# A fused state-space convolution and attention kernel: another order of the setup, fifteen angles and complex products, ranked streams, and shorter VectorE passes

## The chip, the cores and the metric

The kernel runs on one core of a Trainium2 chip. The core has five engines with their own instruction queues: TensorE (PE) for matmuls, VectorE (DVE), ScalarE (ACT), GpSimd (POOL) and SyncE (SP); the last two here only start DMA transfers. The metric is the device time of one execution in microseconds, the median over runs; lower is better.

## The reference

Two independent results are put side by side in the output.

```python
# a: a diagonal state-space model, D = 576 channels, N = 128 states, L = 2048 positions
P = exp(dt * A * l);  K[d, l] = Re( sum_n C[d,n] * P[d,n,l] * dt * B[d,n] )
a = causal_convolution(u, K) + u * Dskip          # over rfft/irfft of length 2L
# b: attention with 32 query heads of 18, and one key and one value head; S = 2048
q = x @ wq;  k = x @ wk;  v = x @ wv
b = softmax(q k^T / sqrt(18)) v  @ wo
out = concat([a, b], -1)
```

## The kernel before, in words

**Attention.** Four chunks of 512 queries, 16 pairs of heads in each, 16 blocks of 128 keys: 1024 score steps. A step is two matmuls of one head each (`s`, two times 128 keys x 512 queries, float16 operands in two parts), one exponential on ScalarE of 128 x 1024 (`P`, lines 741 and 743), and its share of the product with the values (`ops`, float32, four column groups at once). Scores have three PSUM buffers, so they are issued in groups of three; the exponentials of a group free the buffers for the next. Between groups TensorE does other work through one PSUM bank (`bank`): products, query projections (`q`), output projections (`op`), and the matmuls of the convolution. Whatever goes through that bank has to be copied out by VectorE before the next can begin.

**Convolution.** Twelve groups of 48 channels. For each, `factors` builds powers of exp(dt A) for 26 positions a channel and state: a magnitude (an exponential on ScalarE) times a cosine and a sine (two ScalarE sine passes); `tables` multiplies them up to a table `tab` of 2 x 24 x 96 for each half group, `kgen` (`kg`) contracts the table over states on TensorE into the filter. The input and the filter are transformed by matmuls with DFT matrices (`hu`, `lu`, `hk`, `lk`), multiplied with a three-way splitting on VectorE and by accumulating DMAs (`spectrum`, `back`), and transformed back (`iy`). Two channel groups share one turn of sines: the second one's arrays are parked in DRAM and fetched back. Since an exponential and a sine need different ScalarE tables, a turn is: two exponentials over 1248 elements, later a table load, four sines of 1248, a table load. There are five such turns in the loop and one in the setup.

**What sets the order.** `build` writes the order of PE, ACT, DVE and POOL by hand, by a planner that keeps an estimated clock for every engine. `main` goes through the score steps; in front of each group `fill` asks the streams for work until the score buffers are expected free. The convolution has four streams (`fronts`, `inputs`, `kernels`, `backs`); `Conv.go` advances the one that has spent the least VectorE work so far. Constants at the head of the file hold the planner's prices and thresholds.

**The setup.** It loads weights and x, projects the first queries (`kq`, copied to `qc`), places them (`rows`), projects keys (`kv`) and values (`pv`) for the whole sequence in four column groups, and places the first keys (`kaug`). It also runs the arguments and sines of the first two channel groups. The bound on the scores needs the keys' maxima (`km`, `kmx`, `kmax`) and a matmul `up`. After the first two scores the loop places the second keys (`kp`), finishes the value projection, transposes the values (`vp`) to `v_sb`, and computes the other four maxima (`kmx`, four 128-wide matmuls).

## Time and profile before

| | |
|---|---|
| runs | 1161.06, 1162.67, 1165.83 us; median 1162.67 |
| profiled execution | 1167.64 us; its span, first to last instruction, 1165.9 us |
| busy PE, ACT, DVE, POOL | 1102.5, 1038.6, 924.4, 97.4 us (95%, 89%, 79%, 8%) |
| mean granted TensorE clock | 0.988 |
| DMA | 123.93 MB, a mean of 106 GB/s |

A row of the groups reads: line, engine, operation, output and inputs with shapes, count, then busy time and mean duration in ns, then the engine's idle time just before and who ended it. A line number is often that of a helper (291 is the one that records every matmul, 326 the two-operand VectorE operation), so the names tell the groups apart. A float32 matmul shows as two rows of the profile. A row of the timeline starts with the start in us from the span's beginning and the time until the last of the merged instructions ends; the next one can start a little before that. In brackets stands the idle time in front.

### The profile page before, as it was taken

To read this page: it belongs to the slowest core of one execution; us is meant where nothing else is said; L and a number is where in the kernel's file an instruction comes from. 1 tells how busy PE (TensorE), PEld (TensorE's weight loads), DVE (VectorE), ACT (ScalarE), POOL (GpSimd) and SP (SyncE) were. 2 spreads that over 40 slices of the span, in tenths; PEclk is the share of its full clock that TensorE was granted. 3 is DMA by queue.
4 is the path that set the end of the run, shared out by engine and by line. 5 is a ranking of instruction groups with operands and counts; after the bars stand their busy time and mean duration, and the time that the engine had idled before them with its cause. 6 is when DMAs were issued, how large, how long until landed. Compare 5 with 4: busy or idle time off the path is not lost. (4 is left out here: it accounts for less than half of the span.)

```text
span 1165.9 us, 42886 instructions
## 1 busy us (share of the span) xinstructions
PE 1102.5 (95%) x18790; PEld 563.4 (48%) x18790; DVE 924.4 (79%) x1649; ACT 1038.6 (89%) x1092; POOL 97.4 (8%) x151
## 2 busy tenths in 40 slices
PE   7999999999998899999899999899999899998997
PEld 2454554454445455455444445455455455554444
DVE  7686886985896896797997697896799888796643
ACT  5798999999987999899998998999999999997983
POOL 2001110201010100010120000000110100000000
PEclk9899999999998999999999999999999999999999
DMA  8323261524242353143554133352234252243141
GB/s 307 125 70 117 85 171 52 164 76 124 89 115 79 129 125 112 43 96 99 155 141 154 47 66 94 126 127 99 84 67 139 77 154 83 72 95 99 47 91 57
DMA packets 55026, 123.93 MB, mean 106 GB/s; under 512 B 7500, under 2 KB 24925, under 8 KB 53555
## 3 DMA queue, kind: packets, MB, share of 16 engines
q1 hardware_dynamic: 43571, 87.44, 21.7%
q0 software_dynamic: 10832, 33.27, 13.5%
q8 instruction: 149, 2.44, 0.9%
q10 hardware_dynamic: 432, 0.44, 0.1%
q14 instruction: 42, 0.34, 0.1%
HBM read 53.47 MB, written 41.46 MB: 81 GB/s over the span
## 5 line engine op out<-in xcount | busy, mean ns | idle before, releaser
L743 ACT ACTIVATE P<-s 128x1024 f32<-128x1024 f32 x992 | 942.0, 1027 | 91.3 <-PE s L291 87.3
L291 PE MATMUL ops<-P,v_sb 128*32 128x256 f32 (+1 forms) x9008 | 550.2, 364 | 8.1 <-DVE o L330 6.0
L291 PEld LDWEIGHTS ops<-P,v_sb 128*32 128x32 f32 x9008 | 271.5, 110 | 218.5 <-issue 74.6
L291 PE MATMUL s<-aug,kaug 55*128 55x512 f16 x2048 | 292.7, 381 | 11.3 <-ACT P L743 5.8
L291 PEld LDWEIGHTS <-kaug 55*128 55x128 f16 x2048 | 95.0, 94 | 185.1 <-issue 137.6
L291 PE MATMUL op<-wo_sb,oT 126*32 126x288 f32 (+1 forms) x1120 | 85.4, 428 | 8.7 <-DVE ob L330 5.1
L291 PE MATMUL q<-x,wq_sb 128*32 128x256 f32 x1360 | 87.1, 388 | 6.2 <-DVE ql L346 3.9
L291 PEld LDWEIGHTS q<-x,wq_sb 128*32 128x32 f32 x1360 | 42.2, 111 | 41.4 <-issue 16.9
L326 DVE TENSOR_TENSOR tab<-tab,tt 128x576 f32<-128x576 f32 (+1 forms) x72 | 59.1, 821 | 1.8
L326 DVE TENSOR_TENSOR tab<-tab 128x576 f32<-128x576 f32 (+1 forms) x72 | 58.6, 814 | 0.0
L326 DVE TENSOR_TENSOR ks<-ks 128x384 f32<-128x384 f32 (+2 forms) x84 | 55.1, 668 | 1.6
L291 PEld LDWEIGHTS op<-wo_sb,oT 126*32 126x32 f32 (+1 forms) x1120 | 35.3, 114 | 43.0 <-issue 10.2
L276 POOL DMA_DIRECT2D qd<-qh x46 | 26.0, 578 | 322.7 <-DVE qh L334 322.7
L291 PE MATMUL kg<-tab 128*32 128x64 f32 x2304 | 42.9, 224 | 9.7 <-DVE us L326 7.5
L326 DVE TENSOR_TENSOR acc<-acc 128x768 f32<-128x768 f32 (+1 forms) x48 | 40.2, 854 | 11.3 <-DMA acc<-t 10.5
L291 PEld LDWEIGHTS kg<-tab 128*32 128x32 f32 x2304 | 36.8, 112 | 23.9 <-issue 15.2
L326 DVE TENSOR_TENSOR t<-us,ks 128x1728 f32<-128x1728 f32 (+2 forms) x36 | 47.2, 1347 | 0.0
L334 DVE TENSOR_SCALAR qh<-q 128x256 f16<-128x256 f32 x34 | 14.1, 416 | 37.3 <-PE q L291 37.3
L741 ACT ACTIVATE P<-s,nb 128x1024 f32<-128x1024 f32 x32 | 33.3, 1114 | 8.1 <-PE s L291 8.0
L276 POOL DMA_DIRECT2D ks<-ks x12 | 11.0, 914 | 332.9 <-DVE ksb L330 224.4
L330 DVE COPY ksb<-kg 128x192 f32<-128x192 f32 x48 | 17.2, 359 | 26.5 <-PE kg L291 26.5
L326 DVE TENSOR_TENSOR us<-us 128x384 f32<-128x384 f32 (+1 forms) x60 | 37.1, 633 | 1.0
(356 smaller groups left out, 1076.7 us busy)
## 6 DMA issues: line engine op xcount, KB each, us to landing
park<-two SPq DMA_DIRECT2D x6, 1944.0 KB
acc<-t POOLq DMA_DIRECT2D x12, 864.0 KB, 6.8
od<-o SPq DMA_DIRECT2D x31, 256.0 KB
acc<-t POOLq DMA_DIRECT2D x12, 576.0 KB, 5.7
aug<-qd SPq DMA_DIRECT2D x124, 54.0 KB
u<-u SPq DMA_DIRECT2D x12, 384.0 KB
kd<-ksb SPq DMA_DIRECT2D x12, 384.0 KB
kt<-kd SPq DMA_DIRECT2D x48, 96.0 KB
```

The source lines that it names most:

```text
L276: return self.q.dma_start(out, src, **k)
L291: return self.e.matmul(out, w, x, **k)
L326: return self.v.tensor_tensor(out, a, b, **k)
L330: return self.v.tensor_copy(out, src)
L334: return self.v.tensor_scalar(out, src, *a, **k)
L741: nc.scalar.activation(pt, ps, AF.Exp, scale=SCALE / UNIT ** 2, bias=self.nb)
L743: nc.scalar.activation(pt, ps, AF.Exp, scale=SCALE / UNIT ** 2)
```

## The change

Line numbers shift by a few lines (291 becomes 296, 326 becomes 331, 743 becomes 749). The parts are these.

- **Angles.** 15 positions a channel instead of 26 go through the arguments, exponential and sines; the other 11 come as complex products of those (six VectorE operations over 288 elements and six over 144). Parked arrays shrink with it. The buffer of one array is shared with another.
- **Setup.** Raw parameters of group 0 go first on SP's queue, those of group 1 on ScalarE's. The keys' projection takes its pieces in another order; two value projections move behind the third score, and all five maxima move ahead of the first score, as matmuls in column groups. The value copy and transposes, and the second placement, move in the order shown below.
- **Streams.** `Conv.go` ranks by work divided by a share: 6.88 for `fronts`, about 0.92 for `inputs` and `kernels`, 1.46 for `backs`.
- **Pieces.** The two long passes of `back` (1728 and 1152 elements) become three and two operations; the sum in `factors` two.
- The planner's constants change, and the output buffer `ob` gets two copies. The order of everything in the loop follows from these.

```diff
-LAND_G = 1.7
-LOAD = 1.15
+LAND_G = 1.7501
+LOAD = 1.1638
...
 NF = 26
+NB = 15
...
+WF = 6.8815
+WI = 0.9251
+WK = 0.9218
+WB = 1.4569
...
-        for k in (0, 1):
+        for k in (0, 1, 4):
             project(kps, 0, k)
-            project(pv, 32, k)
-        for k in (4, 2, 3):
+        for k in (2, 3):
+            project(pv, 32, k - 2)
             project(kps, 0, k)
+        self.place, self.spread, self.put, self.km = place, spread, put, km
+        V.tensor_copy(kc, kps)
         project(pv, 32, 4)
-        V.tensor_copy(kc, kps)
...
-        pk = self.bank(4, "kmx")
-        nc.tensor.matmul(pk, spread[:, 0:P], km[:, 0:4], start=True, stop=True)
+        pk = kv[:, 0, 0:4]
+        matmul4(nc, pk, spread[:, 0:P], km[:, 0:4])
+        self.maxima()
...
-        self.last = lambda: project(pv, 32, 3)
+        self.last = lambda: [project(pv, 32, k) for k in (2, 3)]
...
-            if i == 1:
-                self.late_setup()
-                self.second()
             if i == 2:
                 self.values()
-                self.maxima()
+            if i == 4:
+                self.second()
...
-        shp = [P, ND, NF]
+        shp = [P, ND, NB]
...
-        tt(r, r, m, op=mu)
-        yield "v", 0.0, False
-        tt(f, f, m, op=mu)
-        yield "v", 0.0, False
+        im, re = self.im, p1.tile(shp, F32, tag="r", name=f"r{k}_")
+        lo = lambda t, a, b: t[:, :, 0:16].rearrange("p c (g x) -> p c g x", x=8)[:, :, :, a:b]
+        four = lambda t: t[:, :, 0:8].rearrange("p c (g x) -> p c g x", x=4)
+        for t, x in ((re, r), (im, f)):
+            tt(lo(t, 1, 5), four(x), four(m), op=mu)
+            tt(t[:, :, 16:20], x[:, :, 8:12], m[:, :, 8:12], op=mu)
+            tt(t[:, :, 20:25:2], x[:, :, 12:15], m[:, :, 12:15], op=mu)
+            V.memset(t[:, :, 0:16:8], 1.0 if t is re else 0.0)
+            yield "v", 0.0, False
+        for size, base, by, to in (([P, ND, 2, 3], lambda t: lo(t, 1, 4), lambda t: lo(t, 4, 5), lambda t: lo(t, 5, 8)),
+                                   ([P, ND, 3], lambda t: t[:, :, 20:25:2], lambda t: t[:, :, 19:20], lambda t: t[:, :, 21:26:2])):
+            t1 = p1.tile(size, F32, tag="tmp", name=f"e1_{k}_{len(size)}")
+            t2 = p1.tile(size, F32, tag="dif", name=f"e2_{k}_{len(size)}")
+            br, bi = by(re).broadcast_to(size), by(im).broadcast_to(size)
+            tt(t1, base(im), bi, op=mu)
+            tt(to(re), base(re), br, op=mu)
+            tt(t2, base(im), br, op=mu)
+            yield "v", 0.0, False
+            tt(to(im), base(re), bi, op=mu)
+            tt(to(re), to(re), t1, op=sb)
+            tt(to(im), to(im), t2, op=ad)
+            yield "v", 0.0, False
...
-        tt(sm, r, f, op=ad)
-        yield "v", 0.0, False
+        for h in (slice(0, ND // 2), slice(ND // 2, ND)):
+            tt(sm[:, h], r[:, h], f[:, h], op=ad)
+            yield "v", 0.0, False
...
-            for h in (slice(0, 4), slice(8, 12), slice(4, 8)) if m == 0 else (slice(0, 12),):
+            for h in ((slice(0, 4), slice(8, 12), slice(4, 8)), (slice(0, 4), slice(4, 8), slice(8, 12)), (slice(0, 6), slice(6, 12)), (slice(0, 12),))[m]:
...
+        self.load(0, nc.sync)
         nc.scalar.dma_start(self.con, self.a["con"])
-        self.load(0, nc.scalar)
-        self.load(1, nc.gpsimd)
+        self.load(1, nc.scalar)
...
-        for st in sorted(self.streams, key=lambda st: (not st.holds, st.work)):
+        for st in sorted(self.streams, key=lambda st: (not st.holds, st.work / st.share)):
```

How the order moves is seen best on TensorE at three places. The first is the end of the setup, from the placing of the keys (`kq<-kc`) to the matmul of the bound (`up`, which is the last `kv<-aw` row in the change). Before:

```order
L291 MATMUL kq<-kc,place_sb 32x512 x4
L291 MATMUL kmx<-km,spread_sb 128x4
L291 MATMUL pv<-x_130,wkv_sb 32x512
L291 MATMUL pv<-xr,wkv_sb 32x512 x3
L291 MATMUL up_0_300<-aw_0_290,all 32x8 x4
```

And in the change:

```order
L296 MATMUL kq<-kc,place_sb 32x512 x4
L296 MATMUL kv<-km,spread_sb 32x4 x4
L296 MATMUL kmx_290<-km,spread_sb 32x4 x16
L296 MATMUL kv<-aw_0_310,all 32x8 x4
L296 LDWEIGHTS kaug
```

A value projection (`pv`) has left this place, and the four other maxima (sixteen matmuls) have come.

The second is the ramp, on TensorE behind the first two scores before, and behind the third in the change (`s_1_1` is head pair 1, key block 1). Before:

```order
L291 MATMUL kp_356<-kc,place_sb 32x512 x4
L291 MATMUL pv<-x_130,wkv_sb 32x512
L291 MATMUL pv<-xr,wkv_sb 32x512 x3
L291 LDWEIGHTS kaug
L291 MATMUL s_0_1_374<-aug_111,kaug 128x512
L291 LDWEIGHTS kaug
L291 MATMUL s_0_1_374<-aug_111,kaug 128x512
L295 MATMUL vp<-ident,keys 128x128 x4
L291 MATMUL kmx_383<-km,spread_sb 128x4 x4
```

And in the change:

```order
L296 MATMUL pv<-x_130,wkv_sb 32x512
L296 MATMUL pv<-xr,wkv_sb 32x512 x3
L296 LDWEIGHTS kaug
L296 MATMUL s_1_1_388<-aug_112,kaug 128x512
L296 LDWEIGHTS kaug
L296 MATMUL s_1_1_388<-aug_112,kaug 128x512
L296 LDWEIGHTS kaug
L296 MATMUL s_0_2_397<-aug_111,kaug 128x512
L296 LDWEIGHTS kaug
L296 MATMUL s_0_2_397<-aug_111,kaug 128x512
L296 MATMUL kp_400<-kc,place_sb 32x512 x4
L300 MATMUL vp<-ident,keys 128x128 x4
```

The scores come closer together, and the transposes (`vp`) stand behind the placement of the second keys (`kp`); the four wide `kmx` matmuls are gone from here.

The third is the first sine turn of the loop: what TensorE has between the score group that is issued as the sines begin and the next one. Before (products, the bound, two groups of a query projection):

```order
L291 MATMUL ops_5_2986<-P_10_4_3061,v_sb 32x256 x2
L291 MATMUL ops_5_2986<-P_11_4_3066,v_sb 32x256 x2
L291 MATMUL ops_5_2986<-P_10_4_3061,v_sb 32x128 x2
L291 MATMUL ops_5_2986<-P_11_4_3066,v_sb 32x128 x2
L291 MATMUL up_1_3145<-aw_1_3084,all 32x8 x4
L291 MATMUL up_1_3145<-aw_0_2201,all 32x1 x4
L291 MATMUL q_2_0_3164<-x_1738,wq_sb 32x256 x20
L291 MATMUL q_2_1_3192<-x_1738,wq_sb 32x256 x20
```

And in the change:

```order
L296 MATMUL ops_4_2612<-P_8_15_2948,v_sb 32x256 x2
L296 MATMUL ops_4_2612<-P_9_15_2990,v_sb 32x256 x2
L296 MATMUL q_1_1_3069<-x_2346,wq_sb 32x256 x20
L296 MATMUL ops_5_3106<-P_10_0_3003,v_sb 32x256 x2
L296 MATMUL ops_5_3106<-P_11_0_3008,v_sb 32x256 x2
L296 MATMUL ops_5_3106<-P_10_0_3003,v_sb 32x256 x2
L296 MATMUL ops_5_3106<-P_11_0_3008,v_sb 32x256 x2
L296 MATMUL up_1_3124<-aw_1_3100,all 32x8 x4
L296 MATMUL up_1_3124<-aw_0_2728,all 32x1 x4
L296 MATMUL ops_5_3106<-P_10_1_3046,v_sb 32x256 x2
L296 MATMUL ops_5_3106<-P_11_1_3051,v_sb 32x256 x2
```

One projection group instead of two stands in this turn, and more products.

More of the change, by code (lines that the diff above doesn't have):

```diff
@@ L346, in scalar_tensor_tensor, with memset @@
         return self.v.scalar_tensor_tensor(out, a, x, b, **k)
[L348 to L349 removed]
+    def memset(self, out, x):
+        self.k.v += 0.07
+        return self.v.memset(out, x)
 class Stream:
@@ L579, in second @@
         K.pe(0.86, ps)
[L580 to L600 removed]
+        vp = self.ps_o.tile([P, CT], F32, tag="o", name="vp").rearrange("p (j n) -> p j n", j=4)
         for j in range(4):
@@ L603, in values, with maxima, maxima_end @@
         K.pe(1.0, vp)
+        to = self.kaug[:, CT:2 * CT]
+        V.tensor_scalar(to, ps, self.spread[:, FLAG + 6:FLAG + 7], None, op0=ALU.add)
         V.tensor_copy(self.v[:, :, :DH].rearrange("p (c j) d -> p c j d", j=4), vp.rearrange("p j (c d) -> p c j d", c=4)[:, :, :, :DH])
+        self.o_free = K.v + HOP + 0.03
+        self.put(to, ps, 0)
         K.filled()
+    def maxima(self):
+        pk = self.bank(16, "kmx4")
+        for m in range(1, 5):
+            matmul4(self.nc, pk[:, 4 * m - 4:4 * m], self.spread[:, 2 * m:2 * m + P] if m < 4 else self.spread[:, 136:136 + P], self.km[:, 0:4])
+        self.pk = pk
+    def maxima_end(self):
+        V, pk = self.V, self.pk
+        V.tensor_reduce(self.kmax[:, 1:5], pk.rearrange("p (m c) -> p m c", c=4), axis=AX.X, op=ALU.max)
+        V.tensor_scalar(self.kmax[:, 1:5], self.kmax[:, 1:5], FLOOR, None, op0=ALU.max)
     def load_wo(self):
@@ L1289, in frame @@
         w = p1.tile([P, 3, ND], F32, tag="w", name=f"w{k}")
-        f, r, m = (p1.tile([P, ND, NF], F32, tag=t, name=f"{t}{k}_") for t in ("f", "r", "sum"))
+        f, m = (p1.tile([P, ND, NB], F32, tag=t, name=f"{t}{k}_") for t in ("tmp", "sum"))
+        self.im = p1.tile([P, ND, NF], F32, tag="f", name=f"f{k}_")
+        r = self.im.rearrange("p c n -> p (c n)")[:, :ND * NB].rearrange("p (c n) -> p c n", n=NB)
         return w, f, r, m
```

113 lines of the change are left out of this document (48 added, 65 removed).

## The prediction

> **What bounds the kernel now.** I read the engine totals first, then who waits for whom, then three stretches: the start, one of the five places where ScalarE computes sines, and the tail.
>
> ```profile
> PE 1102.5 (95%) x18790; PEld 563.4 (48%) x18790; DVE 924.4 (79%) x1649; ACT 1038.6 (89%) x1092; POOL 97.4 (8%) x151
> L743 ACT ACTIVATE P<-s 128x1024 f32<-128x1024 f32 x992 | 942.0, 1027 | 91.3 <-PE s L291 87.3
> PE s L291 <- ACT P L743: 5.8, 16, 0.5
> PE kg L291 <- DVE us L326: 7.5, 4, 3.1
> PE ops L291 <- DVE o L330: 6.0, 11, 1.3
> PE op L291 <- DVE ob L330: 5.1, 3, 2.7
> 25.63:38.16 12.53, 10.68 (x81) 4.90 (x82) 9.68 (x23) 6.36 (x6) 1.18 (x3) 0.73 0.75 259
> 30.87:37.70 6.83, 6.78 (x50) 3.82 (x54) 4.83 (x8) 3.13 (x3) 0.00 (x0) 0.50 0.85 296
> 38.16:1148.00 1109.84, 1059.54 (x18364) 546.16 (x18360) 887.00 (x1570) 1017.20 (x1068) 91.38 (x136) 0.99 0.35 101
> 1148.00:1166.00 18.00, 12.03 (x190) 7.07 (x188) 8.00 (x14) 1.10 (x3) 0.00 (x0) 0.95 0.20 70
> ```
>
> TensorE is the bound, with ScalarE close behind. The exponentials wait 87.3 us for scores, while scores wait only 5.8 us for exponentials. In the stage table (columns: length, then busy PE, weight loads, DVE, ACT, POOL, granted clock, DMA) TensorE works 1059.5 of the 1109.8 us of the steady part. So time can come only from what TensorE loses: waits, most of them for a VectorE evacuation queued behind longer work, half-clock time, and stretches in which ScalarE does something other than exponentials. TensorE's own work hardly changes: counted over the program, scores, projections and transforms are the same; 160 half-width `ops` matmuls become 80 full ones.
>
> **The change, part by part.** Four terms carry the sum: the start (A), the sine blocks (B), the tail (C), VectorE's load (D).
>
> *A, the start.* TensorE, ScalarE and VectorE rows from the first 40 us:
>
> ```profile
> 11.62 1.24 ACT L280 ACTIVATE two<-two 128x1248 f32<-128x1248 f32 x1 [2.13 <-DVE two L326]
> 12.77 0.58 ACT L280 ACTIVATE qc<-kq 128x512 f32<-128x512 f32 x1
> 22.22 1.06 PE L291 MATMUL kq<-kc,place_sb 128*32 128x512 f32 x8
> 22.72 1.28 ACT L280 ACT_TABLE_LOAD   x1
> 24.12 0.67 ACT L280 ACTIVATE kaug<-kq,spread_sb 128x512 f16<-128x512 f32 x1
> 25.63 0.60 PE L291 MATMUL s<-aug,kaug 55*128 55x512 f16 x4 [0.94 <-DVE kaug L346]
> 26.17 1.06 PE L291 MATMUL kp<-kc,place_sb 128*32 128x512 f32 x8
> 29.71 0.66 PE L295 MATMUL vp<-ident,keys 128*128 128x128 f32 x4 [1.30 <-DVE keys L330]
> 30.92 1.87 PE L291 MATMUL kmx<-km,spread_sb 128*128 128x4 f32 x8 [0.55 <-DVE v_sb L330]
> 32.73 1.46 PE L291 MATMUL s<-aug,kaug 55*128 55x512 f16 x6
> 38.16 0.82 PE L291 MATMUL s<-aug,kaug 55*128 55x512 f16 x6
> 33.38 3.13 ACT L741 ACTIVATE P<-s,nb 128x1024 f32<-128x1024 f32 x3 [3.80 <-PE s L291]
> 38.59 12.52 ACT L741 ACTIVATE P<-s,nb 128x1024 f32<-128x1024 f32 x12 [2.09 <-PE s L291]
> ```
>
> The first score (25.63) waits for `kaug`, and that for ScalarE: the placed keys are done at 22.22 + 1.06 = 23.28, but the table load and what precedes it hold ScalarE until 24.12, a loss of 0.84. Before that, `qc` waits until 12.77 behind an exponential of 1248 elements, though its projection ends near 11.8: some 0.7 more. With 720 elements both are gone, and since the projections between them run back to back I take 1.5 us in all. The added 16 small `kmx` matmuls stand ahead of the first score, in the shadow of that `kaug` copy.
>
> Then the ramp. Three exponentials run, ScalarE sits 3.80 us, three run, it sits 2.09. TensorE waits 1.30 and 0.55 for VectorE copies, spends 1.87 on `kmx`, and runs at half clock from 30.87 to 37.70. In the new order three scores come at once, the value projections (0.86 each) fill the time of the first exponential, `kmx` is past, and the transposes come after the keys' placement, when the copy they need is done. Stepping through the new rows with these durations: first score 24.1, exponentials from 24.5, the seventh score (two matmuls each) near 29.8 instead of 38.16, 8.4 us ahead. At that point the old order has done more `ops` and `q` work, 1.7 us of it. So A = -6.7 us; I use **-6.5**. Some 3.4 of it is half-clock time (6.83 x 0.5), which would come back if TensorE is again too idle there, so A lies between -3 and -8. The key loads on SP's queue stand behind the parked arrays, which shrink; raw data now goes ahead of the first weights on that queue, one issue (about 0.45 us), which is inside the margin of A.
>
> The Trainium skill ("TensorE: Matmul & The Clock Gate", Part 1) says that the clock falls to half after one idle window of about 3.4 us, and asks for no gap over some 3 us. The trace differs: the longest gap in front of a TensorE row here is 1.30 us and still 6.83 us went at 0.50. By the page the dip would need another cause, the change need not remove it, and A would be about -3.1.
>
> *B, the sine blocks.* Five times ScalarE leaves the exponentials for sines. The first of them, ScalarE, then TensorE:
>
> ```profile
> 209.22 2.85 ACT L743 ACTIVATE P<-s 128x1024 f32<-128x1024 f32 x3 [0.20 <-PE s L291]
> 212.10 1.28 ACT L280 ACT_TABLE_LOAD   x1
> 213.39 1.24 ACT L280 ACTIVATE f__2696<-f__2696 128x1248 f32<-128x1248 f32 x1
> 218.24 1.28 ACT L743 ACT_TABLE_LOAD   x1
> 219.53 2.86 ACT L743 ACTIVATE P<-s 128x1024 f32<-128x1024 f32 x3
> 211.79 0.82 PE L291 MATMUL s<-aug,kaug 55*128 55x512 f16 x6
> 212.54 0.86 PE L291 MATMUL ops<-P,v_sb 128*32 128x256 f32 x16
> 215.12 4.05 PE L291 MATMUL q<-x,wq_sb 128*32 128x256 f32 x40 [1.41 <-DVE un L338]
> 220.27 2.37 PE L291 MATMUL q<-x,wq_sb 128*32 128x256 f32 x40 [1.10 <-DVE ql L346]
> 222.57 0.60 PE L291 MATMUL s<-aug,kaug 55*128 55x512 f16 x4
> ```
>
> From 212.10 to 219.53, 7.43 us, no exponential runs; scores are 10.78 us apart (211.79 to 222.57), and the next come when the exponentials of 219.53 end. TensorE has only about 6.1 us to do (two `q` groups of 2.2, `ops` and `up` 0.8, scores 0.95), so it loses 4.7 whatever its waits are. The four sines take 218.24 - 213.39 = 4.85, 1.21 each; 720 of 1248 elements at that rate, rounded up for the fixed part, is 0.75. That saves 1.85 a block, and two exponentials of the same width before it 0.88: 2.73, times five 13.6 us of ScalarE. It is not all time. By the order, with 0.43 for a full product (0.86 for the sixteen rows at 212.54; a matmul shows as two rows), 0.43 a `q` step (2.2 / 5), and 0.49 an `op` step and 0.34 a transform step (rows under C), TensorE finds 28.9 us of work in the five old blocks and 23.5 in the new; these 5.4 us are done elsewhere at TensorE's price. What is left, 8.2, holds only where ScalarE ends the block last. I take half, **-4**, ends 0 and -13.6.
>
> *C, the tail.* Counted from the program, the last chunk's output sums left for after the last exponential rise from 12 steps to 15. At 0.49 us a step (eight rows of the chain of waits, the second below; the first has two transform steps) that is +1.5:
>
> ```profile
> 1133.90 0.68 PE iy L291 x16
> 1139.61 0.49 PE op L291 x8
> ```
>
> They leave the loop, but its last 17 score groups then hold less TensorE work than exponentials, so the loop does not shorten there. The last inverse transforms stand before score 972 instead of 1014, so no convolution ends late. **+1.5**, ends 0 and +2.
>
> *D, VectorE.* Fewer angles against complex products and smaller pieces:
>
> ```profile
> 33.12 1.45 DVE L326 TENSOR_TENSOR r__192<-r__192,sum__193 128x1248 f32<-128x1248 f32 x1
> 34.49 1.45 DVE L326 TENSOR_TENSOR f__191<-f__191,sum__193 128x1248 f32<-128x1248 f32 x1
> 35.86 0.55 DVE L326 TENSOR_TENSOR t<-r__192,w 128x384 f32<-128x384 f32 x1
> 36.33 0.55 DVE L326 TENSOR_TENSOR t<-f__191,w 128x384 f32<-128x384 f32 x1
> L326 DVE TENSOR_TENSOR t<-us,ks 128x1728 f32<-128x1728 f32 x12 | 23.4, 1948 | 0.0
> ```
>
> Start to start, 1248 elements cost 1.37 us and 384 cost 0.47: 1.04 ns an element and 0.07 fixed. For one channel group, three two-operand passes over the angles lose 528 elements each and the two magnitude products 2496; the new products have 1440 and the complex ones 6 x 288 + 6 x 144 = 2592, so the elements cancel to 48. Two one-operand passes lose 528 each at about half the price, -0.56. The instructions rise by 22 (4 and 2 in the magnitudes, 12 in the complex products, 1 in the sum, 3 in the products with the spectrum), 22 x 0.07 = +1.54. So +1.0 a group, +12 us of VectorE in twelve groups, 924 to some 936, still under TensorE. Against it, the 1.95 us pass that an evacuation can wait behind becomes three of about 0.67. The rows cannot tell which wins: bounds -8 (a quarter of TensorE's roughly 30 us of waits for VectorE) and +12 (each added microsecond waited for). I take **0**; the ranking of streams moves which work stands where, and I count it here at nothing, since the work per score group comes out the same on average.
>
> The Trainium skill ("VectorE: DVE Perf Modes", the section on the TRN2 errata) speaks against D: each instruction pays its fixed part, by its formula for this operation 151 cycles, 0.157 us, and tiles under 512 elements are to be avoided. By that estimate 22 x 12 instructions add 41 us and D's VectorE load rises by 35. The rows agree with it for a lone operation (384 elements, 0.55) but not in a queue (0.47 apart); no row yet shows the new short forms.
>
> **Sum:** -6.5 - 4 + 1.5 + 0 = -9.0 us against the profiled execution's own 1167.64 (span 1165.9 and 1.7 around it), so 1158.6. That execution is 5.0 over the three runs' median of 1162.67; for the median I predict 1153.7.
>
> **Rivals.** *Only the start, and half of it*: the half clock stays, and the blocks end as late as before, because TensorE (with waits like the 2.7 for `ob`) and not ScalarE is last. Then -3 to -5 + 1.5, near 1160. For it: five blocks in which evacuations also wait. Against it: in the block shown ScalarE is plainly last. *Larger*: the pieces also take 8 us off the waits and the full 8.2 of B arrives: 1162.67 - 6.5 - 8.2 - 8 + 1.5 = 1141.5. For it: the longest waits (3.1, 2.7) lie behind long passes or DMA landings. Against it: those behind landings stay. *Slower*: VectorE's 264 added instructions delay the evacuations that TensorE waits for; every added microsecond is paid (+12) and the shorter blocks drown in it (B = 0): -6.5 + 12 + 1.5 = +7, 1169.7. It decides once these waits pass 15 us more than today's. For it: 79% VectorE, one PSUM bank for everything that is not score or product. Against it: 21% idle, and shorter operations ahead. *The ramp does not come*: the value projections now lie between scores, and if the projection of the keys waits for its inputs, the first score stays at 25.6; that is inside the first rival.
>
> **How the numbers follow.** Forecast (1146 to 1156.5) 0.56; larger 0.11; only the start 0.22; slower 0.11. About 0.5% (5.8 us) is what a measurement of this kernel can tell from no change. Faster: 0.56 + 0.11 = 0.67; same 0.22; slower 0.11. Adding all ends would give -31 to +12; the range takes the forecast, the small case and the upper part of the larger one, **1143 to 1163**.
>
> **What would show it.** A: first score near 24.1, exponentials without a gap over 0.5 us until 40, no 0.50 clock between 25 and 40. B: no-exponential stretches of 5.6 us instead of 7.4. C: last exponential to end about 1.5 us longer. D: VectorE near 936 busy, and waits of TensorE for it no higher in sum. It is wrong if the half clock appears in the ramp, if TensorE's waits for VectorE rise by over 10 us, or if the seventh score comes after 33.

## The result, and the profile after

The changed kernel takes **1152.47 us** (median of 6 runs, 1149.98 to 1157.21). The kernel before, on the same chip, takes 1165.01 (6 runs; the three known ahead of the prediction had 1162.67). The ratio is **0.9894, 95% interval 0.9868 to 0.9920**: about 1.1% faster, which is more than the 0.5% that a measurement can tell. The forecast was 1153.7, range 1143 to 1163. The total was right; most of the terms in it were not, and what follows is mainly about that. One run of e3 (below), 3662.83 us where its other eleven took 1157.40 to 1163.90, is left out of its median.

The profiled execution of the changed kernel took 1157.21 us with a span of 1155.0, 4.7 above its median; the one of before was 5.0 above the median of the three runs known ahead of the prediction. Its page, the first waits of TensorE, and the stages (start, steady part, tail) of the changed kernel; the columns are those of the views of before:

```profile
PE 1096.4 (95%) x18660; PEld 556.4 (48%) x18660; DVE 935.8 (81%) x1910; ACT 1021.8 (88%) x1092; POOL 96.4 (8%) x150
```

```profile
PE s L296 <- ACT P L749: 7.4, 22, 0.5
PE ops L296 <- DVE o L335: 7.1, 7, 4.6
PE iy L296 <- issue: 6.8, 2, 5.8
PE up L296 <- DVE aw L339: 4.3, 3, 2.5
```

```profile
25.60:38.20 12.60, 11.33 (x165) 4.37 (x164) 10.95 (x38) 10.77 (x11) 3.04 (x6) 1.00 0.61 209
38.20:1135.60 1097.40, 1051.48 (x18152) 538.91 (x18147) 902.90 (x1823) 999.49 (x1065) 90.89 (x136) 0.99 0.34 93
1135.60:1155.10 19.50, 13.44 (x212) 8.07 (x212) 8.20 (x14) 0.77 (x2) 0.00 (x0) 0.96 0.18 65
```

ScalarE is busy 16.8 us less, VectorE 11.4 us more (935.8; forecast some 936). All rows of TensorE's waits added up, those for VectorE fall from 41.8 to 28.9 us, while those put down to "issue" (the view names no releaser) rise from 2.7 to 8.1. The longest of these, 5.79 us before an `iy`, ends when VectorE's last write of `acc` does, so the waits for VectorE fall by some 7 rather than 12.9. TensorE's busy time falls by 6.1 and its idle time by 4.8; together that is the 10.9 of the span. Some 3.5 of the 6.1 is clock and not work: with the slow rows at the start (last section) TensorE worked 30.8 us at half rate before and 23.9 after.

**Where the time went.** The 1024 exponentials on ScalarE are a clock for the whole program. I cut the span at their starts: the first one, the thirteenth (number 12, counted from 0), 48 exponentials around each of the five sine turns, everything else between the thirteenth and the last, and from the start of the last to the end.

| profiled execution | first | to number 12 | five turns | rest | tail | span |
|---|---|---|---|---|---|---|
| before | 26.1 | 18.8 | 292.9 | 809.5 | 18.6 | 1165.9 |
| after | 28.0 | 12.4 | 277.9 | 816.2 | 20.5 | 1155.0 |
| difference | +1.9 | -6.4 | -15.0 | +6.7 | +1.9 | -10.9 |

So the start gives 4.5 us, the turns 15, and 8.6 are lost in the rest and the tail. ScalarE's first exponentials in the changed kernel, and above them TensorE's first projection:

```profile
8.33 7.05 PE L296 MATMUL kq<-x,wq_sb 128*32 128x512 f32 x40 [3.16 <-DMA x<-xT]
27.96 9.15 ACT L747 ACTIVATE P<-s,nb 128x1024 f32<-128x1024 f32 x9 [1.30 <-PE s L296]
37.27 9.41 ACT L747 ACTIVATE P<-s,nb 128x1024 f32<-128x1024 f32 x9 [0.15 <-PE s L296]
```

The ramp is as forecast: eighteen exponentials with a gap of 0.15 between them, where the old kernel sat 3.80 and 2.09 us. But it begins 1.9 us later instead of 1.5 earlier, because the projection of the first queries waits 3.16 us for x.

A sine turn of the changed kernel, ScalarE and then the scores around it on TensorE:

```profile
206.98 1.28 ACT L285 ACT_TABLE_LOAD   x1
208.28 0.81 ACT L285 ACTIVATE tmp__2745<-tmp__2745 128x720 f32<-128x720 f32 x1
208.99 0.88 ACT L285 ACTIVATE f__2747<-f__2747,hp_sb 128x720 f32<-128x720 f32 x1
211.37 1.28 ACT L749 ACT_TABLE_LOAD   x1
212.66 2.86 ACT L749 ACTIVATE P<-s 128x1024 f32<-128x1024 f32 x3
206.69 0.82 PE L296 MATMUL s<-aug,kaug 55*128 55x512 f16 x6
215.45 1.46 PE L296 MATMUL s<-aug,kaug 55*128 55x512 f16 x6
```

From 206.98 to 212.66 no exponential runs: 5.68 us instead of 7.43, forecast 5.6. The scores are 8.76 us apart instead of 10.78.

Not all of the 15 us in the turns is ScalarE's. In the five windows TensorE was busy 273.1 us before, 13.7 of it at half clock, and 263.2 after, 3.4 of it at half clock. At half clock half the work is done, so the 15.0 are 5.1 of clock, 5.1 of idle time (19.8 to 14.7), and 4.7 of work that now stands elsewhere. How much of the clock's part is there in every run is open: the profiled execution of before has a mean clock of 0.988, while the medians over the runs are alike (0.992 before, 0.991 after).

And a loss that the old kernel does not have, in the order VectorE, GpSimd, TensorE, ScalarE:

```profile
154.93 1.83 DVE L331 TENSOR_TENSOR acc<-acc 128x768 f32<-128x768 f32 x2 [5.53 <-DMA acc<-t]
147.97 0.86 POOL L281 DMA_DIRECT2D acc<-t  x1 [10.28 <-DMA t<-t]
161.40 1.51 PE L296 MATMUL iy<-acc,dft_sb 128*32 128x192 f32 x16 [5.79 <-issue]
164.83 2.85 ACT L749 ACTIVATE P<-s 128x1024 f32<-128x1024 f32 x3 [7.91 <-PE s L296]
160.30:167.10 6.80, 5.70 (x54) 2.68 (x58) 6.45 (x11) 2.27 (x3) 0.64 (x1) 0.50 0.43 144
```

An accumulating transfer is issued at 147.97, VectorE waits for it until 154.93, and VectorE's writes of `acc` last until 161.30. TensorE, whose next instruction in the written order is the inverse transform of that group, sits 5.79 us; scores stand behind it, so ScalarE sits 7.91. Then, by the last row, the clock is at 0.50 for 6.8 us. There is a second place at 348, where VectorE stands behind another transfer (`db<-rden`). Between the starts of two exponentials lie 9.0 and 7.1 us there; outside the turns the old kernel has one gap of that kind, 6.2. The two places cost some 9 us more than that one. With the 4.7 us of work moved out of the turns that is more than the +6.7 of "rest", so something else in the loop was gained; no run says what.

### The profile page after: what moved, and what is told of

Read it like the earlier page. It is cut to its first block, busy times and chain, and to the rows that moved or that the text cites. A ratio compares the mean times of both kernels' runs of the same rounds, so it can differ in the third digit from the quotient of the medians.

```text
span 1155.0 us, 42904 instructions
## 1 busy us (share of the span) xinstructions
PE 1096.4 (95%) x18660; PEld 556.4 (48%) x18660; DVE 935.8 (81%) x1910; ACT 1021.8 (88%) x1092; POOL 96.4 (8%) x150
## 5 line engine op out<-in xcount | busy, mean ns | idle before, releaser
L296 PEld LDWEIGHTS ops<-P,v_sb 128*32 128x32 f32 x8848 | 267.9, 110 | 212.5 <-issue 72.2
L296 PE MATMUL op<-wo_sb,oT 126*32 126x288 f32 (+1 forms) x1096 | 79.3, 408 | 2.1 <-DVE out L335 2.1
L331 DVE TENSOR_TENSOR t<-us,ks 128x576 f32<-128x576 f32 x72 | 50.4, 753 | 0.0
L281 POOL DMA_DIRECT2D acc<-t x24 | 20.7, 863 | 254.9 <-PE s L296 66.0
L331 DVE TENSOR_TENSOR acc<-us,ks 128x768 f32<-128x768 f32 x36 | 32.6, 953 | 4.6 <-DMA ks<-ks 4.6
L331 DVE TENSOR_TENSOR us<-lu,scu 128x384 f32<-128x384 f32 x48 | 24.4, 550 | 14.3 <-PE lu L296 14.3
```

The lines of the kernel that those rows point to most:

```text
L281: return self.q.dma_start(out, src, **k)
L296: return self.e.matmul(out, w, x, **k)
L331: return self.v.tensor_tensor(out, a, b, **k)
```

## The experiments

Two kinds. Four keep every engine's written order and change a duration or a queue (e1, e2, e3, e5): they price a term by itself. Eight change a part or a constant, and the planner writes another order for the loop (e4, e6 to e12). The kernel before, run beside them, had medians of 1164.09 (e1 to e4), 1164.77 (e5 to e8) and 1164.70 (e9 to e12); e5 to e8 ran on another chip than the other experiments. All are cut at the exponentials as above:

| kernel | time, median | ratio to before, 95% | first | to 12 | turns | rest | tail |
|---|---|---|---|---|---|---|---|
| before | 1165.01 | | 26.1 | 18.8 | 292.9 | 809.5 | 18.6 |
| after | 1152.47 | 0.9894 (0.9868 to 0.9920) | 28.0 | 12.4 | 277.9 | 816.2 | 20.5 |
| e1 old load queues | 1153.29 | 0.9885 (0.9847 to 0.9923) | 25.5 | 12.4 | 277.8 | 816.4 | 20.4 |
| e2 longer turns | 1171.48 | 1.0055 (1.0031 to 1.0078) | 28.3 | 12.4 | 296.7 | 813.5 | 20.4 |
| e3 more VectorE | 1161.24 | 0.9970 (0.9946 to 0.9993) | 26.4 | 12.4 | 280.0 | 822.3 | 20.4 |
| e4 after, one constant moved | 1177.74 | 1.0107 (1.0071 to 1.0143) | 27.6 | 12.4 | 291.3 | 813.8 | 27.5 |
| e5 before, shorter turns | 1163.20 | 0.9983 (0.9969 to 0.9996) | 26.8 | 17.2 | 291.6 | 809.1 | 19.1 |
| e6 before, one constant moved | 1167.89 | 1.0018 (1.0005 to 1.0031) | 27.7 | 17.2 | 295.5 | 802.2 | 24.3 |
| e7 setup only | 1178.52 | 1.0111 (1.0093 to 1.0129) | 25.8 | 14.0 | 297.9 | 818.3 | 24.6 |
| e8 angles only | 1186.40 | 1.0191 (1.0167 to 1.0216) | 25.8 | 17.2 | 279.4 | 811.8 | 47.4 |
| e9 angles and ranking | 1189.75 | 1.0236 (1.0196 to 1.0276) | 25.5 | 15.6 | 281.2 | 840.1 | 23.5 |
| e10 after, no ranking | 1193.68 | 1.0254 (1.0234 to 1.0273) | 26.7 | 12.4 | 280.4 | 812.3 | 58.2 |
| e11 after, long passes | 1203.32 | 1.0345 (1.0320 to 1.0371) | 26.6 | 12.4 | 289.8 | 844.5 | 25.4 |
| e12 after, old setup | 1164.69 | 0.9997 (0.9980 to 1.0015) | 25.6 | 15.6 | 286.8 | 811.8 | 21.5 |

Segments come from one execution each. Before, e5 and e6 have the same order in their first groups and need 18.8, 17.2 and 17.2 to number 12, so a segment of the start scatters by some 1.6 us.

**e1: the raw loads on their old queues.** The order of the loop is that of the changed kernel.

```diff
-        self.load(0, nc.sync)
         nc.scalar.dma_start(self.con, self.a["con"])
-        self.load(1, nc.scalar)
+        self.load(0, nc.scalar)
+        self.load(1, nc.gpsimd)
```

> The changed kernel with one thing undone: the raw parameters of groups 0 and 1 are loaded again from ScalarE's and GpSimd's queues, so that the first weights and x head SP's queue as before. The order of everything in the loop stays as it is in the changed kernel. Theory 1 (the start was mis-sized because x came late): in the changed kernel the first projection waits 3.16 us for x and starts at 8.33 instead of 5.68 us, at half clock; with this the first score should come near 24 us instead of 27.5, and the total fall by about 3 us against the changed kernel's 1152.5. Theory 2 (the first score is bound by the keys' projection or ScalarE anyway): first score within 1 us of 27.5, total within 1 us.

1153.29 us, not to be told from the changed kernel, as Theory 2 has it; but the first score comes at 25.09 instead of 27.53, between the two theories. In the trace the start is 2.4 us earlier, and the lead is kept to the end (the span is 1152.5). TensorE, then ScalarE, of e1:

```profile
5.48 1.92 PE L296 MATMUL kq<-x,wq_sb 128*32 128x512 f32 x16 [0.61 <-DMA x<-xT]
8.61 2.78 PE L296 MATMUL kq<-x,wq_sb 128*32 128x512 f32 x24 [1.20 <-DMA x<-xT]
20.54 0.63 PE L296 MATMUL kv<-xr,wkv_sb 128*32 128x512 f32 x3 [0.54 <-DMA xr<-xT]
25.52 9.15 ACT L747 ACTIVATE P<-s,nb 128x1024 f32<-128x1024 f32 x9 [1.30 <-PE s L296]
```

The projection waits 1.81 us in all instead of 3.16, and its forty rows need 4.70 instead of 7.05, so it ends 4.0 us earlier. Of these some 1.5 are lost again: the keys' projection stands at 20.54 for the last piece of x (its weight load waited 1.44 us). All six kernels profiled with the raw data first on SP's queue wait 2.7 to 3.5 us there and have their first exponential between 26.4 and 28.3; with the old queues seven of eight wait at most 2.1 in all, e6 2.12 at once, and the first exponential is at 25.5 to 27.7. So the new queue costs the start about 1.2 us on average (27.3 against 26.1; against e1 and e7 alone, which have the new setup too, 1.6). Whether the old queues gain anything in the median is not shown.

**e2: ScalarE's turns made longer again.** Two exponentials and four sines over 440 elements, on data that nothing reads, are added to each turn without the planner counting them. The order stays.

```diff
...
+            def pad(func, n):
+                for _ in range(n):
+                    self.nc.nc.scalar.activation(rest, self.hp.broadcast_to([P, 440]), func)
...
                 nc.scalar.activation(m2, m2, AF.Exp)
+                pad(AF.Exp, 2)
...
                 sines(r2, f2)
+                pad(AF.Sin, 4)
```

> The changed kernel with ScalarE's work at the five sine turns put back to about what it was for 26 angles, by idle activations of 440 elements (0.44 us each, their result is not used): two behind the two exponentials, four behind the four sines, 5 x 6 x 0.44 = 13.2 us of ScalarE in all. No other engine's order changes. Theory 1 (term B, as forecast): about half of the 13.2 us is time: 5 to 8 us slower than the changed kernel. Theory 2 (ScalarE ends these blocks, all of it is time): 11 to 13 us slower, which would be the whole gain of the change. Theory 3 (TensorE ends them): within 1.5 us of the changed kernel.

1171.48, 19 us above the changed kernel, more than any of the three theories, for 15.5 us more of busy ScalarE by the page (1037.3; 13.2 were meant). The table shows it where it was put: the turns take 296.7 instead of 277.9. ScalarE in the first turn of e2, and the head of TensorE's waits:

```profile
210.53 2.35 ACT L1322 ACTIVATE two<-hp_sb 128x440 f32<-128x440 f32 x4
212.89 1.28 ACT L749 ACT_TABLE_LOAD   x1
214.19 2.85 ACT L749 ACTIVATE P<-s 128x1024 f32<-128x1024 f32 x3
```

```profile
PE ops L296 <- ACT P L749: 10.1, 8, 2.6
PE s L296 <- ACT P L749: 9.0, 26, 0.5
```

In the new order ScalarE ends the turn last, in all five of them (2.8 to 4.8 us longer each). The price comes in two parts. TensorE idles 23.9 us in the five windows instead of 14.7; its waits for ScalarE rise from 9.3 to 20.0 in all. And it does 18.7 us of its work there at half clock instead of 3.4. The fourth turn, changed kernel and e2, with the same 956 rows of TensorE (length, TensorE's busy time, weight loads, VectorE, ScalarE, GpSimd, clock, DMA):

```profile
670.52:725.34 54.82, 54.26 (x956) 28.78 (x950) 51.03 (x116) 52.71 (x59) 4.11 (x5) 1.00 0.44 119
677.55:737.13 59.58, 55.98 (x956) 28.92 (x950) 51.12 (x116) 55.90 (x65) 4.12 (x5) 0.97 0.41 110
```

This is no chance of one execution: the twelve runs of e2 have a mean clock of 0.979 to 0.988, the seven of the changed kernel 0.988 to 0.994.

**e5: ScalarE's turns made shorter in the old order.** The mirror of e2: the kernel before, with its exponentials and sines in the loop's turns over the first 720 of 1248 elements. The other elements stay untransformed, so the filter is another one; the work of all other engines, and the order, are the old ones.

```diff
-                nc.scalar.activation(m, m, AF.Exp)
-                nc.scalar.activation(m2, m2, AF.Exp)
+                def fewer(x, func, **kw):
+                    K.act(0.07 + ND * NF / 1.2e3, x, (x,), func)
+                    x = x.rearrange("p c n -> p (c n)")[:, :ND * 15]
+                    self.nc.nc.scalar.activation(x, x, func, **kw)
+                fewer(m, AF.Exp)
+                fewer(m2, AF.Exp)
...
-                sines(r, f)
-                sines(r2, f2)
+                for cos, sin in ((r, f), (r2, f2)):
+                    fewer(sin, AF.Sin, scale=TWO_PI)
+                    fewer(cos, AF.Sin, scale=-TWO_PI, bias=self.hp)
```

> The kernel before, every engine's instructions in their old order, but the two exponentials and four sines of the convolution's five turns in the loop work on the first 720 of 1248 elements (the rest of each array stays untransformed, so the filter is another one). This is part B of the change alone: ScalarE loses 2.7 us a turn, 13.6 in all; VectorE and TensorE do the same as before. Theory 1 (with the order fixed, ScalarE's time at the turns is paid in full both ways): 10 to 14 us less than before, near 1152. Theory 2 (prediction: half of it is hidden because TensorE's waits end the block): 4 us less, near 1160. Theory 3 (it only costs when added, because the order was fitted to the old durations): 0 to -2.

1163.20 against 1164.77: 1.6 us of the 13.6 (13.2 by the page), so Theory 3 holds, Theory 1 falls, and even the halved term of the prediction is too much for this order. The fourth turn shows why. ScalarE and TensorE of e5, and then of before:

```profile
742.05 1.28 ACT L743 ACT_TABLE_LOAD   x1
743.34 2.86 ACT L743 ACTIVATE P<-s 128x1024 f32<-128x1024 f32 x3
750.51 2.85 ACT L743 ACTIVATE P<-s 128x1024 f32<-128x1024 f32 x3 [4.31 <-PE s L291]
740.72 2.61 PE L291 MATMUL op<-wo_sb,oT 126*32 126x288 f32 x40
746.03 3.84 PE L291 MATMUL op<-wo_sb,oT 126*32 126x288 f32 x32 [2.70 <-DVE ob L330]
```

```profile
750.61 2.86 ACT L743 ACTIVATE P<-s 128x1024 f32<-128x1024 f32 x3
755.12 2.86 ACT L743 ACTIVATE P<-s 128x1024 f32<-128x1024 f32 x3 [1.65 <-PE s L291]
750.64 3.69 PE L291 MATMUL op<-wo_sb,oT 126*32 126x288 f32 x32 [2.69 <-DVE ob L330]
```

The exponentials are free earlier, but ScalarE then sits 4.31 us for scores instead of 1.65: TensorE still has its two output projections of the long turn to do, with the 2.7 us for the one `ob` buffer between them, and the second at half clock in both kernels (3.84 and 3.69 us for 32 rows, where the forty before took 2.61). In this order TensorE is last in that turn, and no time comes out. Of the five turns the first two are 1.1 and 0.9 us shorter over their 48 exponentials, the other three +0.6, 0.0 and 0.0. The first two lost one stretch of half clock each (3.4 us) and the third gained one, so even these differences are the clock's; TensorE idles 20.7 us in the five, before 19.8.

**e3: more VectorE in the new order.** 24 products of 384 elements, whose result is overwritten, are added in the convolution, 11.2 us by the page.

```diff
+            if lo == 0:
+                self.nc.nc.vector.tensor_tensor(t[:, :16], L(sm)[:, :16], H(r)[:, :16], op=ALU.mult)
```

> The changed kernel with 24 more VectorE operations of 384 elements, one in the tables of each half channel group (the output is overwritten by the next operation): 24 x 0.47 = 11.3 us of VectorE. No order changes. Theory 1 (term D: VectorE's load as such is hidden): within 2 us of the changed kernel. Theory 2 (each added microsecond of VectorE is waited for): 8 to 11 us slower; then the cheaper part of the change would have cost as much and the rest would have gained more than 20.

1161.24, 8.8 us above the changed kernel, as Theory 2 has it (8 to 11); in the trace the last exponential starts 6.5 us later although the first was 1.6 earlier, so 8.1. TensorE's waits for VectorE rise from 28.9 to 35.6. So VectorE's 81% is no reserve: with the order fixed, an added microsecond at these places costs 0.7 to 0.8 us.

**e4 and e6: one constant moved.** The same work in another order: HOP, a hand-over price of the planner, 0.0401 to 0.0430 in the changed kernel, 0.075 to 0.078 in the kernel before.

> The changed kernel with one constant of the planner moved a little (its allowance for the hop between engines, 0.0401 to 0.043), which means nothing for the hardware but lets the planner put out another order of the loop (2517 of about 7000 rows of TensorE's order differ). It measures how much of a difference comes from the order alone. If the gain of the change lies in its mechanisms, this stays within 3 us of the changed kernel; if it lies in a lucky order, it can fall back by 5 to 12 us.

> The kernel before with one planner constant moved by 4% (HOP 0.075 to 0.078): same work, another order from about the twentieth score group on. It measures how much of a difference is the order's alone. Theory 1 (the constants of each kernel are fitted to it, so that any other order loses): 5 to 15 us slower than before, near 1173, as the same step on the kernel after cost 25. Theory 2 (orders scatter on both sides): within 5 us of before, either sign.

The changed kernel loses 25 us, more than its expectation allowed, and is slower than before; the kernel before loses 3, as its Theory 2 has it. Between two orders of the same work there can be more than the whole gain of this change. e4 loses 13.4 in the turns and 7 in the tail, with waits like those of the changed kernel, only more of them.

**e7, e8: one part of the change alone on the kernel before.** e7 has the new setup, e8 the 15 angles; each with the old constants, and the loop is planned anew.

```diff
 e8:
+NB = 15
...
-        shp = [P, ND, NF]
+        shp = [P, ND, NB]
...
```

> The kernel before with the new order of the setup alone (projection order, values and second placement later, five maxima ahead of the first score; old load queues, 26 angles, old constants); the loop is planned anew. Theory 1 (the setup is worth what the trace of after shows where the raw loads are on the old queues): first exponential near 25.5, seventh score near 31, exponentials 4 to 6 us ahead of before around the hundredth, the total changed by -5 plus what the new plan of the loop costs (0 to +15). Theory 2 (the early lead is lost again within the first turn): no lead at the hundredth exponential.

> The kernel before with 15 angles and complex products alone (old setup, old pass lengths, old constants); the loop is planned anew. ScalarE loses 13.6 us, VectorE gains 18 instructions a channel group, some 10 us. Theory 1 (both are paid nearly in full): the two cancel, -4 plus what the new plan costs (0 to +15), so 1159 to 1174. Theory 2 (ScalarE's part is gained, VectorE's hidden): -10 or more, below 1153.

Both are slower than before, by 14 and 22 us, outside the totals of their first theories. e7's start is near the forecast: the first exponential comes at 25.8, the seventh score at 33.0 instead of 31, and number 12 is reached 5 us earlier than before (25.8 + 14.0 against 26.1 + 18.8). But at the hundredth exponential the lead is 0.4 us, so Theory 2 holds there; the turns, the rest and the tail then each lose 5 to 9 by the new order. e8's table row is the surprise: its last exponential starts at 1134.2, 13.1 us before the old kernel's and level with the changed one's 1134.5, its turns take 279.4, but its tail 47.4. TensorE of e8 at its end:

```profile
1157.86 1.51 PE L292 MATMUL iy<-acc,dft_sb 128*32 128x192 f32 x16 [21.51 <-DVE acc L327]
```

The gain in the turns is there with the angles alone, and with the one `ob` buffer of the old kernel. It is lost because the last channel group of the convolution comes after the last exponential, and TensorE waits 21.51 us for its spectrum.

**e9, e10: the ranking of the streams.** e9 is e8 with the new ranking; e10 is the changed kernel with all shares 1.

```diff
 e9:
...
-        for st in sorted(self.streams, key=lambda st: (not st.holds, st.work)):
+        for st in sorted(self.streams, key=lambda st: (not st.holds, st.work / st.share)):
...
 e10:
-WF = 6.8815
-WI = 0.9251
-WK = 0.9218
-WB = 1.4569
+WF = 1.0
+WI = 1.0
+WK = 1.0
+WB = 1.0
```

> The kernel after with all four shares set to 1, so that the stream with the least work goes first, as before; the loop is planned anew. The last inverse transforms then stand behind the last score. Theory 1 (the ranking keeps the convolution in time): TensorE waits some 20 us for the last group's spectrum after the last exponential, tail 45 us instead of 20, total near 1178; the last exponential itself within 5 us of 1134. Theory 2 (the ranking is worth nothing, as predicted): within 6 us of the kernel after, 1147 to 1158.

> The kernel before with the 15 angles and the ranking of the streams by shares (old setup, old pass lengths, old constants otherwise); the loop is planned anew. In the order, the last inverse transforms stand before score 990, where with the angles alone they stood behind the last score, and 29 output steps are left for the tail instead of 23. Theory 1 (the angles' gain is in the loop, and the ranking decides whether the convolution's last group comes in time): last exponential again near 1134, from there 23 to 25 us to the end, so 1158 to 1162. Theory 2 (the ranking only moves work, the loss returns elsewhere): last exponential after 1145, total above 1168.

e10: without the ranking the last exponential even comes 2.7 us earlier (1131.8; 1.3 of it is an earlier start), and the tail is 58.2 instead of 20.5. That is Theory 1, with a longer tail than its 45. TensorE of e10 at the end:

```profile
1162.42 1.51 PE L296 MATMUL iy<-acc,dft_sb 128*32 128x192 f32 x16 [28.51 <-DVE acc L331]
```

So the ranking does not make the loop faster; it decides whether the convolution is through before the scores are. In e9 it does that too: the tail is back at 23.5, inside the 23 to 25 expected. Yet the total is no better than e8's: its "rest" is 28 us longer, against Theory 1, which had the last exponential at 1134 (it came at 1162.4). Most of that is one place (two gaps of 18.6 and 10.6 us between exponentials), TensorE and then ScalarE of e9:

```profile
1039.99 2.37 PE L296 MATMUL q<-x,wq_sb 128*32 128x256 f32 x40 [0.58 <-DVE ob L335]
1043.45 2.37 PE L296 MATMUL q<-x,wq_sb 128*32 128x256 f32 x40 [1.10 <-DVE ql L351]
1048.01 0.31 PE L296 MATMUL up<-aw,all 128*32 128x8 f32 x16 [2.19 <-DVE aw L339]
1064.11 1.03 PE L296 MATMUL s<-aug,kaug 55*128 55x512 f16 x3 [9.77 <-DMA aug<-sd]
1049.09 4.94 ACT L749 ACTIVATE P<-s 128x1024 f32<-128x1024 f32 x5 [17.55 <-PE ops L296]
```

The query projections had been left until the next heads' scores could not be issued without them. From the last score at 1030.02, three output projections (until 1039.4), the two query projections of the view and the bound stand in a row; ScalarE sits 17.55 us, and then TensorE 9.77 more for the DMA that brings the queries' bound. That the streams of the convolution pushed them back is argued from the edit. The planner's thresholds for urgent work should keep them in time; they are the old ones here. That they are the cause is argued, not shown.

**e11, e12: the change without one part.** e11 has the long passes back whole, e12 the old setup with its load queues; all else, the constants too, as in the changed kernel.

```diff
 e11:
-            for h in ((slice(0, 4), slice(8, 12), slice(4, 8)), (slice(0, 4), slice(4, 8), slice(8, 12)), (slice(0, 6), slice(6, 12)), (slice(0, 12),))[m]:
+            for h in (slice(0, 4), slice(8, 12), slice(4, 8)) if m == 0 else (slice(0, 12),):
```

> The kernel after with the two long passes of the spectrum's products (1728 and 1152 elements) whole again, 3 VectorE instructions fewer a channel group; the loop is planned anew, last inverse transforms before score 999, 32 output steps left plus one op for the tail instead of 23, some 4.5 us. Theory 1 (pieces save TensorE's waits behind the 1.95 us pass): 4.5 for the tail plus up to 8 for the waits, so 1157 to 1165, and the waits of TensorE for VectorE higher. Theory 2 (pieces save nothing): 1153 to 1157, waits as in after.

> The kernel after with the setup of before (projection order, second placement and values after the second score, maxima behind the third, old load queues), all else as in after; the loop is planned anew, last inverse transforms before score 975. Theory 1 (the setup is worth the 2.9 us that the trace of after shows, or 5 with the raw loads on the old queues): first exponential near 25.5, half clock between 30 and 38 again, total 3 to 6 us above after, 1155 to 1159. Theory 2 (the setup carries most of the gain): 1160 or more.

e11 is 51 us above the changed kernel, outside both theories. The tail is 5 longer, as counted; the rest and the turns lose 40, in stalls of 6 to 14 us each. One of them, VectorE and TensorE of e11:

```profile
637.82 0.69 DVE L331 TENSOR_TENSOR oT<-oT,db 126x512 f32<-126x512 f32 x1 [8.51 <-DMA db<-rden]
639.17 3.21 PE L296 MATMUL ops<-P,v_sb 128*32 128x256 f32 x32 [9.10 <-DVE o L335]
```

That is VectorE standing in its written order behind a transfer, with the evacuation that TensorE needs behind it; a pass of 1.95 us has no part in it. So e11 tells nothing of what the pieces save, only that the order written for them fails without them.

e12 equals the kernel before, 12 us above the changed one: by its total Theory 2 would hold, by its stages it does not. Its start takes 25.6 + 15.6 instead of 28.0 + 12.4, 0.8 more; the rest is 4.4 shorter and the turns are 8.9 longer, 5.6 of that in the last one. The new setup's worth at the start is therefore about 1 us with the raw data first on SP's queue, and about 3.3 with the old queues (e1: 25.5 + 12.4); e7 against before gives 5, and with the scatter of 1.6 us none of the three is sharp. What else lies between e12 and the changed kernel (12 us in the medians, 6 in the profiled executions) is another order of the loop.

## Why the prediction was right

The total was right because an overrated start and underrated turns cancelled, which is luck. By its own steps:

- **A, the start, -6.5: half of it came.** Number 12 starts 4.5 us earlier, of which by the prediction's own figure 1.7 is work that the old order had already done: -2.8, just outside its -3 to -8. The step that failed is "raw data now goes ahead of the first weights on that queue, one issue (about 0.45 us), which is inside the margin of A". It counted the issue and not the 168 KB that then go ahead of x, nor that the first projection then runs at half rate for 5.1 us. The first score was to come at 24.1 and came at 27.5, the seventh at 33.55, past the 33 set as the mark of error. The 1.5 us behind the projection did come (`qc` held up the placement by 0.71 instead of 1.60, and from the placed keys to the first score it is 1.6 instead of 2.4), but the projection ended 3.6 us later. With the old queues (e1) the start is 7.0 earlier at number 12, 5.3 at equal work, near the forecast; but there the projections do not "run back to back": the keys' projection waits for its input, as the last rival had it, and the first score comes at 25.1. The ramp itself was read rightly: no gap, no 0.50 between 25 and 40. But the half clock was no property of the old setup alone: e9 and e12 have that setup and a mean clock of 1.00 from 25 to 40, e5, e6 and e8 0.89, the old kernel's profile 0.77. The old kernel's dip is gone in the changed kernel, and yet the start moved by no more than the -2.8; that this is near the prediction's other figure, -3.1 with the dip left in, is chance.
- **B, the sine blocks, -4: too small, and for the wrong reason.** The stretch without exponentials shrank as computed (5.68, forecast 5.6). The turns give 15.0; if the 5.4 us of TensorE work that the prediction saw moved out of them are taken off again, 9.6 stay, more than the full 8.2. Some 5 of them are half clock, for which the prediction had no term in the turns, though the block that it showed had it (a `q` group at 215.12 took 4.05 us, the next 2.37). The step that failed is "What is left, 8.2, holds only where ScalarE ends the block last. I take half". In the old order ScalarE does not even end half of them last (e5: 1.3 us of the turns), so half was too much there; but the planner knows the shorter turn and gives TensorE less to do in it (4.7 us less in the five windows), and in the new order ScalarE ends all five (e2: 18.8 us for 15.5 added, part of it clock). The rival of waits like the 2.7 us for `ob` was a true description of the old order, not of the new one.
- **C, the tail, +1.5: right**, 1.9. What the prediction did not see is why it is so short: without the ranking the tail is 58.2 (e10).
- **D, VectorE, 0: its load right, its price not.** 935.8 busy, forecast 936. TensorE's waits for VectorE were put at some 30 us in the old kernel and are 41.8 with all rows added; they fell to 28.9 (or 34.7, with the wait for `acc`), where the prediction had asked only that they do not rise. The other estimate, 35 us more of VectorE, did not come: the short products of 288 elements start 0.36 to 0.38 us apart in the changed kernel, near the rows' price. e3 shows that added VectorE time is paid at 0.7 to 0.8 in the new order; at that price the 11.4 us more would have cost some 8 or 9, so the pieces, the ranking, the second `ob` buffer or the new order would have saved more than that. Which of them did is open: taking one away changes the order, and the order's own losses (e11) drown it.
- **The ranking, "I count it here at nothing"**, was the largest omission: 37.7 us of tail in e10, and 23.9 between e8 and e9. The prediction had no term for a convolution that ends too late, though it noted that the last inverse transforms move from score 1014 to 972.

- **The range.** The ends of the four terms add up to -29.6 and +11, not to -31 and +12; the stated range does not use them.

The slower rival, VectorE's added instructions, is not what makes partial versions slow; that is the written order: work that becomes due too late (the tail of e8 and e10, the queries of e9) and engines that stand in order behind a transfer (e11, and at 155 us in the changed kernel itself). Long waits also cost clock: the runs of e7 to e11 have a mean clock of 0.975 to 0.982 (medians), the changed kernel 0.991. The gain of 11 us in the profiles reads as an order in which 13 us of shorter ScalarE can be used, less the places where it cannot; that reading is argued, and e4, e7 and e8 say that the gain is not robust.

What stays open: how much the pieces and the second `ob` buffer (never tried alone) save, what the changed constants do by themselves, how much of the turns' gain is clock in a usual run, and whether the raw loads on their old queues are worth anything in the median (e1 has the same ratio within its interval).

## What to carry to other kernels

Where the order of all engines is written ahead, shortening an operation can buy next to nothing until the order is planned anew (e5: 1.6 of 13.6 us), and lengthening it is paid at once (e2: 19 for 15.5, part of it by the clock); so price a removed operation by asking what the other engine will be given to do in its place, and not by what it does there now. Ask of every stream of side work whether it still ends in time, at its last piece, not on average: that was 24 to 38 us of tail here, more than all terms of the sum. And a part of such a change tried alone, with constants that fit another order, says little of the part: cut the trace by stages and compare those.

## What the runs showed of the hardware

**The first projection runs at half rate until the full clock is granted, and the clock column reads 1.00 where the trace has no clock record.** Windows of the projection's rows alone, changed kernel: length, TensorE's busy time with its rows (one that overlaps two windows counts in both), the weight loads, VectorE, ScalarE, clock, DMA:

```profile
8.30:10.80 2.50, 2.47 (x12) 0.68 (x16) 0.00 (x0) 0.00 (x0) 1.00 1.05 400
10.80:13.30 2.50, 2.50 (x16) 0.68 (x12) 0.00 (x0) 0.00 (x0) 1.00 1.05 389
13.30:15.30 2.00, 2.00 (x20) 0.47 (x12) 0.00 (x0) 0.00 (x0) 1.00 1.06 390
```

By their starts, four rows take 0.85 us until 13.43 and 0.43 from there on. The first clock record of this trace, the full clock, begins at 13.52; before it there is none, and the column's 1.00 there says nothing. In e3, whose records begin before the projection, the column shows the half clock:

```profile
8.00:11.30 3.30, 3.30 (x20) 1.08 (x16) 0.00 (x0) 0.00 (x0) 0.50 1.04 394
11.40:13.80 2.40, 2.40 (x24) 0.63 (x16) 0.00 (x0) 0.00 (x0) 1.00 1.05 387
```

In the seven profiles in which TensorE waited 2.1 us or more between its warm-up matmuls and the projection, the forty rows took 5.8 to 7.3 us; in the seven with 0.2 to 1.2 us, the first sixteen took 1.9 to 2.5 and the other twenty-four 2.78. So a late transfer costs more than its delay: the projection starts 2.85 us later in the changed kernel than in e1 (8.33 against 5.48) and ends 4.0 later (15.38 against 11.39). The Trainium skill ("TensorE: Matmul & The Clock Gate", Part 1) has throttling as the default, released after a window of about 3.4 us of sustained work. The trace agrees in kind: the warm-up matmuls ran at half rate for 3.64 us (16 rows), 3.16 us of idling followed, and another 5.1 us of work passed before the full rate came.

**What brings the half clock in these traces is how little TensorE does in 3.41 us, in one gap or in pieces.** The clock records change on a grid of 3.41 us. I cut the fourteen traces into the windows of that grid. Of those at full clock, 64 have TensorE busy for less than 0.4 of the time, and the half clock follows every one; 4458 have more than 0.62, and it follows none; of the 106 between, it follows 24. The dip of the old kernel's ramp is one of these: in the 3.41 us ahead of it TensorE was busy for 1.61, with no gap over 1.30.

**A long wait in the middle costs more than itself.** After the 5.79 us at 155 to 161 TensorE ran at 0.50 for 6.8 us, busy for 5.7 of them: at full clock that work is 2.85 us.

**Two executions of one order differ at the start by 1 to 2 us** (the first exponential at 28.0, 28.3 and 26.4 in three kernels with the same start) and then run in parallel to within a microsecond for the next ninety-six exponentials. The difference is there when the first projection ends (15.38, 15.75 and 13.80), 12.6 us ahead of the first exponential in each of the three.
